# Two attentions on one core: a local score's eight places laid side by side, weight splits at other steps, and small VectorE pieces at other steps

## The chip, the core and the metric

The kernel runs on one core of a Trainium2 chip. The core has TensorE (PE in the profile: matrix products into PSUM), VectorE (DVE), ScalarE (ACT), GpSimd (POOL) and SyncE (SP, which here only issues transfers between HBM and SBUF). The engines run side by side. Each takes its own instructions strictly in the order in which the program gave them, and an instruction that waits for another engine holds up everything behind it on its own engine. The metric is the device time of one execution in microseconds (us).

## The reference

Two independent attentions over 2048 places with 576 columns, 32 heads of 18 columns; their outputs stand side by side.

```python
def _A_ref(x, wqkv, wo):              # local: 8 keys per place, at distances 0, 2, ... 14
    qkv = (x @ wqkv) ...              # q, k, v of 32 heads
    idx = pos[:, None] - off[None, :] ; mask = idx >= 0
    logits = einsum("bhsd,bhswd->bhsw", q, kg) * scale ; logits = where(mask, logits, -1e9)
    attn = softmax(logits, axis=-1)   # over the 8 keys
    return einsum("bhsw,bhswd->bhsd", attn, vg) ... @ wo
def _B_ref(x, wqkv, wo):              # full softmax attention of all 2048 places
    p = softmax(einsum("bhqd,bhkd->bhqk", q, k) * scale, axis=-1)
    return einsum("bhqk,bhkd->bhqd", p, v) ... @ wo
```

All of it is computed in float32 accuracy; products whose inputs matter most are taken of a high and a low half ("splits": `hi` is the rounded value and `lo` the rest).

## The kernel before

**The first part** (up to about 416 us of the trace) makes q, k and v of both attentions.

**The main loop** has 512 steps, and `step` counts them. B's heads stand in 8 groups of 4, and the queries in 4 blocks of 512; a step takes one group, one block and one of 16 key tiles of 128. So a block of queries has 16 steps, and ends in the steps whose number is a multiple of 16. In a plain step TensorE makes 4 score tiles of 128 x 512, makes 3 products more of the same kind for a later block (their maxima are subtracted from that block's scores), and multiplies the exponentials of the step before by v into the sums `po` (line 898). VectorE takes the maximum of each of the 3 products (lines 256, 258 and 272, tile `mx`), and ScalarE takes the exponentials of the 4 scores (lines 398 and 401). A product's PSUM bank is free again when its maximum has been taken. At a block's end VectorE also copies the sums: `o<-po`, line 908; in that step and the next it may have a reduction to one least value per query, `m<-mx` (line 282), and its transpose `mt<-m` (line 290).

**Attention A** runs beside this, in 8 blocks j of 256 places. Block j has `start = 10 + 55 * j`, and its pieces are placed at steps counted from there:

- `match` (lines 1042 and 1045, from step 5): GpSimd multiplies q with the keys at the 8 distances and adds over the columns. Its last addition, line 1049, writes the local scores `lg`, 128 partitions x 8 distances x 64 places.
- `most` (line 1059, steps 30 to 33): VectorE takes the maximum over the 8 distances, 16 places a piece, into `am`.
- `lower` (line 1065, step 33): GpSimd subtracts it. `exponents` (line 1069, steps 34 and 35, or all at 35 where step 35 also makes A's output): ScalarE. `total` (line 1076, step 36): GpSimd adds over the distances into `as`.
- `inverses` (line 1080, steps 37 and 38): VectorE, 32 places a piece. `share` (line 1083, step 38): GpSimd multiplies by them.
- `weighted` (lines 1090 to 1096, from step 38): GpSimd multiplies by v and adds; `upper` and `rest` (lines 1100 and 1105) split the result, which goes to HBM, comes back transposed, and is multiplied by A's output weights on TensorE in the steps that `TURNS` lists (line 1239; such a step takes about 4.1 us).

What sets the order is the table `agenda`: `plan(start, pieces)` puts each piece under a step's number, and `due()` runs what stands under the present step when TensorE's, VectorE's and ScalarE's own work of the step has been written. So a piece stands in its engine's queue behind that step's maxima, and there is no other scheduler. GpSimd's queue holds no work of the steps themselves: it runs ahead of the steps until a piece has to wait for another engine.

**Output weights.** `load_wo` (line 1000) loads 5 chunks of A's and of B's output weights into tiles `y` (four buffers, shared with the rows of the output) and, 3 steps later, splits each on GpSimd: a cast (line 176) and a subtraction (line 177). A's chunks are loaded at steps 28, 32, ... 44, B's at steps 404, 408, ... 420.

## Time and profile before

| what | value |
|---|---|
| median of 3 runs | 1580.74 us (1580.18 to 1582.28) |
| the profiled execution | 1580.53 us, its span 1578.7 us |
| busy share of the span | PE 99%, DVE 89%, ACT 75%, POOL 61% |
| granted TensorE clock | 1.00 |
| first `po` product of the main loop | 416.3 us |

The profiled execution's time is 1.8 us above its span, and 0.21 us under the median. A busy PE says little: its matmuls are pipelined and their ends are modelled. How long a step takes is seen in the chain of work that ended last, which lists the `po` products of each step with their start: a plain step is 2.00 us.

### The profile page before, as it was taken

To read this page: it belongs to the slowest core of one execution; us is meant where nothing else is said; L and a number is where in the kernel's file an instruction comes from. 1 tells how busy PE (TensorE), PEld (TensorE's weight loads), DVE (VectorE), ACT (ScalarE), POOL (GpSimd) and SP (SyncE) were. 2 spreads that over 40 slices of the span, in tenths; PEclk is the share of its full clock that TensorE was granted. 3 is DMA by queue.
4 is the path that set the end of the run, shared out by engine and by line. 5 is a ranking of instruction groups with operands and counts; after the bars stand their busy time and mean duration, and the time that the engine had idled before them with its cause. 6 is when DMAs were issued, how large, how long until landed. Compare 5 with 4: busy or idle time off the path is not lost.

```text
span 1578.7 us, 34691 instructions
## 1 busy us (share of the span) xinstructions
PE 1570.7 (99%) x13400; PEld 950.1 (60%) x13400; DVE 1397.6 (89%) x2381; ACT 1183.5 (75%) x1918; POOL 966.0 (61%) x820
## 2 busy tenths in 40 slices
PE   9999999999999999999999999999999999999998
PEld 7999998888544444445444445444444454555776
DVE  5299999999999999999999999999999999999433
ACT  7323441211699999999999999999999999898444
POOL 2305852201257997994996995995995997930100
PEclk9999999999999999999999999999999999999999
DMA  9848954523321253253235316423523142234211
GB/s 263 220 131 208 261 183 126 162 75 100 75 56 55 64 115 90 70 141 100 60 88 145 81 47 155 104 61 103 136 58 98 37 109 71 78 118 157 86 39 61
DMA packets 190149, 173.12 MB, mean 110 GB/s; under 512 B 123120, under 2 KB 136944, under 8 KB 188256
## 3 DMA queue, kind: packets, MB, share of 16 engines
q1 hardware_dynamic: 185120, 159.36, 36.3%
q0 software_dynamic: 4032, 10.63, 3.1%
q8 instruction: 105, 1.72, 0.5%
q10 hardware_dynamic: 832, 0.92, 0.2%
q14 instruction: 60, 0.49, 0.1%
HBM read 97.47 MB, written 72.95 MB: 108 GB/s over the span
## 4 chain that ended last, share of the span: by engine, by line
PE 96%; POOL 2%; DMA 1%; DVE 1%; issue 1%; ACT 0%; SPq 0%; POOLq 0%; ACTq 0%; DVEq 0%
PE po L898 31%; PE bank L239 19%; PE bank L498 16%; PE bank L388 10%; PE bank L1239 8%; PE pair L388 7%; PE bank L424 4%; POOL pr L1045 1%; POOL aohi L1042 0%; DMA first<-xb 0%; DMA raw<-wa 0%; DVE mx L256 0%; POOL ks L177 0%; POOL ohi L844 0%; DMA da<-ohi 0%
## 5 line engine op out<-in xcount | busy, mean ns | idle before, releaser
L239 PE MATMUL bank<-ks,qs 54*128 54x256 f32 (+1 forms) x2526 | 755.1, 372 | 1.3 <-DVE mx L256 0.6
L256 DVE TENSOR_REDUCE mx<-bank 128x1 f32<-128x512 f32 x1024 | 679.9, 684 | 59.5 <-PE bank L239 33.5
L239 PEld LDWEIGHTS bank<-ks,qs 54*128 54x128 f32 x2526 | 414.1, 184 | 428.4 <-DVE mx L272 312.5
L398 ACT ACTIVATE e<-bank 128x512 f32<-128x512 f32 x1024 | 611.2, 603 | 72.9 <-PE bank L388 66.0
L898 PE MATMUL po<-ee,v 128*19 128x512 f32 x2048 | 536.7, 599 | 0.0
L898 PE MATMUL po<-e,v 128*19 128x512 f32 x2048 | 531.4, 599 | 0.0
L401 ACT ACTIVATE ee<-pair 128x1024 f32<-128x1024 f32 x478 | 487.7, 1020 | 1.1 <-PE pair L388 0.4
L388 PE MATMUL bank<-qs,ks 56*128 56x512 f32 x1092 | 460.8, 441 | 0.0
L258 DVE TENSOR_REDUCE mx<-bank 128x2 f32<-128x512 f32 x546 | 355.8, 684 | 20.2 <-PE bank L239 7.2
L272 DVE TENSOR_REDUCE mx<-bank 128x2 f32<-128x512 f32 x478 | 326.1, 682 | 0.0
L388 PE MATMUL pair<-qs,ks 56*128 56x512 f32 x956 | 248.3, 396 | 0.0
L388 PEld LDWEIGHTS bank<-qs,ks 56*128 56x128 f32 x1092 | 194.4, 183 | 15.6 <-ACT e L398 7.1
L1090 POOL TENSOR_TENSOR pr<-lg,akv 128x1024 f32<-128x1024 f32 x72 | 157.2, 2205 | 0.6
L840 ACT ACTIVATE ohi<-bank 128x512 f32<-128x512 f32 (+1 forms) x56 | 30.6, 595 | 147.5 <-issue 125.5
L388 PEld LDWEIGHTS pair<-qs,ks 56*128 56x128 f32 x956 | 137.8, 185 | 0.0
L898 PEld LDWEIGHTS po<-ee,v 128*19 128x19 f32 x2048 | 69.6, 96 | 109.6 <-issue 109.6
L498 PE MATMUL bank<-xhi,ahi 64*128 64x512 f32 x448 | 116.1, 390 | 0.1
L498 PE MATMUL bank<-xlo,ahi 64*128 64x512 f32 (+1 forms) x448 | 104.1, 392 | 0.2 <-POOL xlo L546 0.2
L498 PE MATMUL bank<-xhi,alo 64*128 64x512 f32 x416 | 102.3, 390 | 0.0
L1042 POOL TENSOR_TENSOR pr<-aq,akv 128x1024 f32<-128x1024 f32 x40 | 87.7, 2199 | 17.0 <-PE bank L239 15.9
L1092 POOL TENSOR_TENSOR pr<-pr 128x512 f32<-128x512 f32 x72 | 91.3, 1293 | 0.6
L546 POOL TENSOR_TENSOR alo<-raw,ahi 128x512 fp32r<-128x512 f32 x13 | 16.8, 1294 | 113.1 <-ACT ahi L545 111.8
(210 smaller groups left out, 2369.5 us busy)
## 6 DMA issues: line engine op xcount, KB each, us to landing
do<-n SPq DMA_DIRECT2D x28, 512.0 KB
da<-ohi SPq DMA_DIRECT2D x52, 256.0 KB
akv<-da SPq DMA_DIRECT2D x64, 175.5 KB
out<-y SPq DMA_DIRECT2D x32, 288.0 KB
qs<-dqk SPq DMA_DIRECT2D x30, 288.0 KB
ks<-dqk SPq DMA_DIRECT2D x30, 288.0 KB
at<-dao SPq DMA_DIRECT2D x64, 128.0 KB
rec<-drec SPq DMA_DIRECT2D x29, 256.0 KB
```

What stands on the lines that cost most here:

```text
L239: return nc.tensor.matmul(ps, qs[rows_, b, p, 128 * t : 128 * t + 128], ks[rows_, p, 512 * k + at : 512 * k + at + n], start=True, stop=True)
L256: nc.vector.tensor_reduce(mx[:, r, p, t, k : k + 1], ps, axis=AX.X, op=ALU.max)
L258: nc.vector.tensor_reduce(mx[:, r, p, t, 2 * k - 2 : 2 * k], ps.rearrange("q (h n) -> q h n", h=2), axis=AX.X, op=ALU.max)
L272: nc.vector.tensor_reduce(mx[:, :, p, t, 2 * k - 2 + i], ps.rearrange("q (h n) -> q h n", h=2), axis=AX.X, op=ALU.max)
L388: nc.tensor.matmul(ps, ks[at, p, 128 * kt : 128 * kt + 128], qs[at, b, p], start=True, stop=True)
L398: nc.scalar.activation(e, ps, AF.Exp, scale=SCALE)
L401: nc.scalar.activation(whole, both_scores[0], AF.Exp, scale=SCALE)
L498: nc.tensor.matmul(ps, a, b, start=start, stop=stop)
L898: nc.tensor.matmul(po[32 * i : 32 * i + 19], vs[g][:, kt, 19 * i : 19 * i + 19], es[i], start=kt == 0, stop=kt == NT - 1)
L1090: nc.gpsimd.tensor_mul(at, ap(st["lg"], (0, 2), (SUB, W), (1, SUB)), window(st["v"], n))
L1092: nc.gpsimd.tensor_add(at[:, :, :4], at[:, :, :4], at[:, :, 4:])
L1239: nc.tensor.matmul(sums_[r], a, b, start=i == 0, stop=i == len(both[r]) - 1)
```

## The change

1. The last addition of `match` no longer writes `lg` (distance, place) but a tile `lgt` (place, distance), so that the 8 scores of a place stand side by side; the masked scores of block 0 are written there too. `most` reads them there: 8 neighbours per place instead of 8 values that lie 64 elements (256 bytes) apart. `lower` reads `lgt` with the distance outermost, that is 8 elements (32 bytes) from one place to the next, and writes `lg` in the old order; what follows is as before.
2. The inverses are taken in three pieces, of 22, 21 and 21 places, instead of two of 32, and so `share` and `weighted` stand one step later.
3. Pieces of `most` and `inverses` that fall on a step whose number is a multiple of 16 move behind it, and what follows moves with them. (The rule has a second case that no step here meets.) Worked out by hand from the new code: the maxima of block j = 1 move from steps 95 to 98 to 97 to 100; of j = 3 the fourth moves from 208 to 209; the inverses of j = 0 go from 47 and 48 to 49, 50 and 51, and of j = 7 from 432 and 433 to 433, 434 and 435. `share` moves by 3 steps in j = 0 and 1, by 2 in j = 3 and 7, and by 1 in the others.
4. A's output weights are loaded and split from step 2 on instead of step 28, B's from step 459 on instead of step 404.

```diff
             if c == DH // 2:
                 st["pr"] = st["prs"][0]
-                lg = st["lg"] = work.tile([128, W, SUB], F32, name="lg", bufs=1)
-                nc.gpsimd.tensor_add(lg, st["pr"][:, 0], st["pr"][:, 1])
+                st["lg"] = work.tile([128, W, SUB], F32, name="lg", bufs=1)
+                by = st["by"] = work.tile([128, SUB, W], F32, name="lgt", bufs=1)
+                nc.gpsimd.tensor_add(by.rearrange("p n w -> p w n"), st["pr"][:, 0], st["pr"][:, 1])
...
-            nc.vector.tensor_reduce(st[name][:, at], st["lg"][:, :, at].rearrange("p w n -> p n w"), axis=AX.X, op=op)
+            nc.vector.tensor_reduce(st[name][:, at], st["by"][:, at], axis=AX.X, op=op)
...
         def lower():
-            nc.gpsimd.tensor_sub(st["lg"], st["lg"], ap(st["am"], (0, W), (1, SUB)))
+            nc.gpsimd.tensor_sub(st["lg"], st["by"].rearrange("p n w -> p w n"), ap(st["am"], (0, W), (1, SUB)))
...
         def inverses(n):
-            half = st["as"][:, 0, SUB // 2 * n : SUB // 2 * n + SUB // 2]
-            nc.vector.reciprocal(half, half)
+            third = st["as"][:, 0, (0, 22, 43)[n] : (22, 43, SUB)[n]]
+            nc.vector.reciprocal(third, third)
...
-        INV = ((37, 0), (38, 1))
-        LOWER, SHARE, MATCH, WEIGHT = 33, 38, 5, 38
+        INV = ((37, 0), (38, 1), (39, 2))
+        LOWER, SHARE, MATCH, WEIGHT = 33, 39, 5, 39
+        start = A_FROM + GAP * j
+
+        def clear(at):
+            while (start + at) % NT == 0 or (start + at) % NT == 1 and start + at not in TURNS:
+                at += 1
+            return at
+
+        def apart_from_ends(pieces):
+            fit = []
+            for at, *args in pieces:
+                at = clear(max(at, fit[-1][0] + 1) if fit else at)
+                if not fit and clear(at + 1) > at + 1:
+                    at = clear(at + 1)
+                fit.append((at, *args))
+            return tuple(fit), fit[-1][0] - pieces[-1][0]
+
+        def behind_by(n, pieces):
+            return tuple((at + n, *args) for at, *args in pieces)
+
+        MOST, late = apart_from_ends(MOST)
+        EXPS, TOTAL, INV = (behind_by(late, p) for p in (EXPS, TOTAL, INV))
+        INV, more = apart_from_ends(INV)
+        LOWER += late
+        SHARE += late + more
+        WEIGHT += late + more
...
-        ("a", woa, 28, [[(0, 128 * c, 128)] for c in range(4)] + [[(64 * r, 512, 64) for r in range(2)]]),
-        ("b", wob, STEPS * (NG - 2) + 20,
+        ("a", woa, 2, [[(0, 128 * c, 128)] for c in range(4)] + [[(64 * r, 512, 64) for r in range(2)]]),
+        ("b", wob, STEPS * (NG - 1) + 11,
```

TensorE's order is the same in both kernels. What moves on the others is shown at two places. On VectorE, before, steps 207 and 208, in block j = 3 (`am` are the local maxima, `mx` the maxima of the steps' own products, `o<-po` the copy of the sums in step 208):

```order
L1059 TENSOR_REDUCE am<-lg 128x16
L282 TENSOR_REDUCE m_83<-mx 128x16
L256 TENSOR_REDUCE mx<-bank_12871 128x1
L272 TENSOR_REDUCE mx<-bank_12865 128x2
L256 TENSOR_REDUCE mx<-bank_12886 128x1
L908 COPY o<-po 128x512
L1059 TENSOR_REDUCE am<-lg 128x16
L290 STREAM_TRANSPOSE mt<-m_83 128x32
L256 TENSOR_REDUCE mx<-bank_12916 128x1
L256 TENSOR_REDUCE mx<-bank_12919 128x1
```

The same place of the changed kernel, from the copy in step 208 on into step 209:

```order
L908 COPY o<-po 128x512
L290 STREAM_TRANSPOSE mt<-m_83 128x32
L256 TENSOR_REDUCE mx<-bank_12921 128x1
L256 TENSOR_REDUCE mx<-bank_12924 128x1
L272 TENSOR_REDUCE mx<-bank_12911 128x2
L256 TENSOR_REDUCE mx<-bank_12944 128x1
L256 TENSOR_REDUCE mx<-bank_12954 128x1
L1143 TENSOR_TENSOR y<-bank_12930,y 128x288
L1060 TENSOR_REDUCE am<-lgt 128x16
L256 TENSOR_REDUCE mx<-bank_12994 128x1
```

The fourth maximum stood right behind the copy; now it stands in step 209, behind an addition for A's output (`y`), and `mt` and the step's `mx` follow the copy at once.

On GpSimd, before, the end of `match` of block j = 7, ahead of its maxima at steps 425 to 428 (`qs`, `ks` are the tiles into which B's output weights are split, from `y`):

```order
L176 CAST qs_3591<-y 126x576
L177 TENSOR_TENSOR ks_3592<-y,qs_3591 126x576
L997 MEMSET y 128x576
L1042 TENSOR_TENSOR aohi<-aq,akv 128x1024
L1045 TENSOR_TENSOR pr<-pr 128x1024
L1045 TENSOR_TENSOR pr<-pr,aohi 128x1024
L1049 TENSOR_TENSOR lg<-pr 128x512
L938 TENSOR_TENSOR n<-o,n 128x512
L176 CAST qs_3591<-y 128x576
L177 TENSOR_TENSOR ks_3592<-y,qs_3591 128x576
L1100 CAST aohi<-ao 128x1152
```

The same stretch of the changed kernel:

```order
L1042 TENSOR_TENSOR pr<-aq,akv 128x1024
L1045 TENSOR_TENSOR pr<-pr,aohi 128x1024
L936 TENSOR_TENSOR o<-o,rec 128x512
L937 CAST n<-o 128x512
L1042 TENSOR_TENSOR aohi<-aq,akv 128x1024
L1045 TENSOR_TENSOR pr<-pr 128x1024
L1045 TENSOR_TENSOR pr<-pr,aohi 128x1024
L1050 TENSOR_TENSOR lgt<-pr 128x8x64
L938 TENSOR_TENSOR n<-o,n 128x512
L1101 CAST aohi<-ao 128x1152
L1106 TENSOR_TENSOR ao<-ao,aohi 128x1152
```

The splits of B's output weights are gone from between the pieces of `match`, so that fewer instructions stand ahead of the local scores.

More of the change, by code (lines that the diff above doesn't have):

```diff
@@ L1047, in match @@
                 st["pr"] = st["prs"][0]
-                lg = st["lg"] = work.tile([128, W, SUB], F32, name="lg", bufs=1)
-                nc.gpsimd.tensor_add(lg, st["pr"][:, 0], st["pr"][:, 1])
+                st["lg"] = work.tile([128, W, SUB], F32, name="lg", bufs=1)
+                by = st["by"] = work.tile([128, SUB, W], F32, name="lgt", bufs=1)
+                nc.gpsimd.tensor_add(by.rearrange("p n w -> p w n"), st["pr"][:, 0], st["pr"][:, 1])
                 if j == 0:
                     for w in range(1, W):
-                        nc.gpsimd.memset(lg[:32, w, : DIL * w], MASKED)
+                        nc.gpsimd.memset(by[:32, : DIL * w, w], MASKED)
         def over_window(op, name, i, of):
@@ L1167, in local @@
         pieces += [(16 + 2 * i, lambda i=i: fetch("v", i)) for i in range(4)]
-        start = A_FROM + GAP * j
         for n in range(2):
```

## The prediction

> **What bounds the kernel now.** I read the page's chain, then the chain in order of time, stretch by stretch, and the timeline where the chain leaves TensorE.

> ```profile
> PE 96%; POOL 2%; DMA 1%; DVE 1%; issue 1%; ACT 0%; SPq 0%; POOLq 0%; ACTq 0%; DVEq 0%
> ```

> TensorE carries 96% of the chain. A change that leaves its work alone can only win the time by which some steps are longer than a plain one. The `po` products in the chain of waits show that; their columns are start, length and instruction. First an undisturbed block end (step 80 begins at 577.90) and an undisturbed one in which A's output is made (208 has this form; here it begins at 1192.96):

> ```profile
> 575.90 0.98 PE po L898 x8
> 577.90 0.99 PE po L898 x8
> 580.08 0.98 PE po L898 x8
> 582.07 0.99 PE po L898 x8
> ...
> 1192.96 0.98 PE po L898 x8
> 1197.05 0.98 PE po L898 x8
> 1199.04 0.98 PE po L898 x8
> ```

> So a plain step takes 2.00, the block end 2.18 and 1.99, the other 4.09 and 1.99. Now the four local maxima of j = 4, which meet nothing else; the maxima of j = 1 around the copy in step 96; those of j = 3 around step 208; and the inverses of j = 7 around step 432:

> ```profile
> 960.68 0.98 PE po L898 x8
> 962.69 0.98 PE po L898 x8
> 964.76 0.99 PE po L898 x8
> 966.85 0.98 PE po L898 x8
> 968.93 0.98 PE po L898 x8
> ...
> 610.35 0.99 PE po L898 x8
> 612.72 0.98 PE po L898 x8
> 614.73 1.05 PE po L898 x8
> 616.81 1.05 PE po L898 x8
> ...
> 847.27 0.98 PE po L898 x8
> 851.70 0.98 PE po L898 x8
> 853.85 0.98 PE po L898 x8
> ...
> 1335.23 0.98 PE po L898 x8
> 1337.70 0.98 PE po L898 x8
> ```

> In j = 4 the first maximum costs nothing (2.01), the next three 0.07, 0.09 and 0.08. In j = 1 the steps take 2.37, 2.01 and 2.08 where the undisturbed end had 2.18, 1.99 and 2.00. In j = 3 they take 4.43 and 2.15 against 4.09 and 1.99. In j = 7 one takes 2.47 against 2.18. The maxima of j = 7 are a case of their own; in the timeline, with the idle time before a row in brackets:

> ```profile
> 1318.14 0.39 DVE L1059 TENSOR_REDUCE am<-lg 128x16 f32<-128x128 f32 x1 [0.49 <-POOL lg L1049]
> 1318.16 1.01 PE L898 MATMUL po<-ee,v 128*19 128x512 f32 x2
> 1318.45 0.68 DVE L258 TENSOR_REDUCE mx<-bank 128x2 f32<-128x512 f32 x1
> 1319.05 0.68 DVE L272 TENSOR_REDUCE mx<-bank 128x2 f32<-128x512 f32 x1
> 1320.84 1.01 PE L898 MATMUL po<-ee,v 128*19 128x512 f32 x2
> ```

> Here VectorE waited 0.49 us for GpSimd's local scores, and the step became 2.68 long. These rows give VectorE's budget as well: maxima start 0.60 apart, so three take 1.80 of the 2.00, and 0.20 is left. The local maximum holds the queue for 0.31 (1318.14 to 1318.45): 2.11, which is the 0.07 to 0.09 seen in j = 4.

> **The change part by part.** *Neighbouring scores.* What the maximum costs in the new layout is not in the trace; the nearest rows by group (mean ns behind the bar) are:

> ```profile
> L1059 DVE TENSOR_REDUCE am<-lg 128x16 f32<-128x128 f32 x32 | 11.9, 373 | 0.5 <-POOL lg L1049 0.5
> L282 DVE TENSOR_REDUCE m<-mx 128x16 f32<-128x96 f32 x32 | 7.8, 243 | 0.4
> L1080 DVE RECIPROCAL as<-as 128x32 f32<-128x32 f32 x16 | 5.5, 343 | 0.0
> ```

> The least value `m` reads neighbours: 96 in 243 ns. A maximum `mx` reads 512 in 684 (the 0.68 above), so 1.06 ns an element, and 128 would take 277: 96 ns less than now. The bounds are 373 (no gain) and 243; I take 277, the row for neighbours being nearest. Then the slot is 0.31 - 0.10 = 0.21, three maxima and it make 2.01, and the 0.24 of such a place goes. I count it for j = 0, 2, 4, 5 and 6: 1.20. In j = 3 two of the three are plain, 0.16, and likewise in j = 7, 0.15.

> *Pieces away from the copy.* j = 1: 0.19 + 0.02 + 0.08 = 0.29 goes. j = 3: 0.34 + 0.16 = 0.50; the fourth maximum goes into step 209, behind A's output, where I cost it at nothing because a single small piece costs nothing (2.01 above). j = 7: 0.29 of the long step; its first inverse no longer stands between the copy and the next `mx`, but another still falls into that step, so I take 0.25. j = 0 gains nothing.

> *Three inverses.* A piece of 32 takes 343 ns, so one of 21 or 22 takes between two thirds of that, 229, and all of it: 0 to 0.34 more VectorE a block. None can be dearer than a maximum of 373, of which a single one cost nothing (2.01 above), and `share` waits for the last in any case. I take nothing; at 343 each, two in a row could cost 0.1 a block, 0.8 in all.

> *B's splits later.* By group on GpSimd:

> ```profile
> L176 POOL CAST qs<-y 126x576 fp32r<-126x576 f32 x4 | 2.7, 664 | 0.0
> L177 POOL TENSOR_TENSOR ks<-y,qs 126x576 fp32r<-126x576 f32 x4 | 5.7, 1421 | 0.3
> L1065 POOL TENSOR_TENSOR lg<-lg,am 128x512 f32<-128x512 f32 x8 | 10.2, 1281 | 42.9 <-DVE am L1059 42.9
> L177 POOL TENSOR_TENSOR mt<-mt 128x32 fp32r<-128x32 f32 x32 | 8.0, 251 | 2.6
> ```

> Four splits of 2.09 stood ahead of the scores of j = 7: 8.3 us. Against that `share` of j = 6 comes a step, 2.0, later. The scores are ready 6.3 us sooner, and the wait of 0.49 is gone: of the step's excess of 0.68 I take 0.67. Next late would be the first inverse, which waits for no such queue. The splits now run at the end of GpSimd's work, where it idles. On SP the five loads pass the transfers of A's last output rows and of B's kept outputs; the `y` buffers they take were last used four allocations earlier, so I cost them at nothing.

> *A's splits earlier.* 10.4 us of GpSimd move from its waits for `am` (42.9 us in all over seven blocks) into an idle stretch at the loop's start. One split stood before the first scores and one still does. Nothing.

> *Share later.* `share` of j = 0 moves by 3 steps, 6.0 us, and GpSimd has no pause between it and the next scores:

> ```profile
> 513.41 1.28 POOL L1083 TENSOR_TENSOR lg<-lg,as 128x512 f32<-128x512 f32 x1 [2.58 <-DVE as L1080]
> 605.39 1.30 POOL L1049 TENSOR_TENSOR lg<-pr 128x512 f32<-128x512 f32 x1
> 612.09 0.37 DVE L1059 TENSOR_REDUCE am<-lg 128x16 f32<-128x128 f32 x1
> ```

> One multiplication of 512 elements by `rec` (1.3, as long as `lower`) now runs in the wait ahead of `share`, so the scores of j = 1 are ready at 606.7 + 4.7 = 611.4. The first maximum now stands in the step in which the third did, at 612.09. It is 0.7 in time; a wait of up to 0.3 would follow if the write in the new order took 1 us more. I take 0.

> *The sum:* 1.20 + 0.16 + 0.15 + 0.29 + 0.50 + 0.25 + 0.67 = 3.22. The profiled execution, 1580.53, becomes 1577.3; it stands 0.21 under the median of the runs, so the forecast is 1577.5.

> **The price of `lower`, and the rivals.** `lower` now reads at 32 bytes distance. ScalarE's exponentials wait for it:

> ```profile
> 502.95 1.28 POOL L1065 TENSOR_TENSOR lg<-lg,am 128x512 f32<-128x512 f32 x1 [4.26 <-DVE am L1059]
> 503.89 0.60 ACT L398 ACTIVATE e<-bank 128x512 f32<-128x512 f32 x1
> 504.37 0.43 ACT L1069 ACTIVATE lg<-lg 128x256 f32<-128x256 f32 x1
> ```

> It ends at 504.23, 0.14 before ScalarE gets to them; a maximum shorter by 0.10 makes that 0.24. So stretches in four blocks (0, 1, 3 and 6; the others have a step more) hurt from 0.24 on, and ScalarE's queue behind it holds the next scores. Bounds from rows: its own 1.28, and 4.0 at the dearest price per element, 251/32 = 7.8 ns (`mt`) for 512. A gain is excluded, since it still writes as many elements as it reads. I take the near row, its own: nothing.

> *Rival 1: `lower` is some tenths longer.* Each 0.1 by which it grows beyond 0.24 costs 4 x 0.1. Between 1.6 and 2.3 us it gives back 0.3 to 3.1: 1577.8 to 1580.6, mostly within 0.2%. [...]

> *Rival 2: the maximum gets no cheaper.* Then 1.20 + 0.31 stay and part of the rest; about 1.5 is won: 1579.2. Against it stands the 243 ns row. [...]

> *Rival 3, slower: `lower` on ScalarE's path in full.* To end 3.2 us above the time before, it has to lose 6.4: 4 x (growth - 0.24) = 6.4, so from 3.1 us on. At the 4.0 of the dear row it loses 4 x 2.48 = 9.9: 1587.4. For it speaks only a 32-element row that is mostly fixed cost.

> *Rival 4:* SP is held by a late `y` buffer at steps 459 to 475, so that A's last transposed rows reach TensorE late. Those loads are issued 9 steps, 18 us, ahead. 1579 to 1584.

> **How the numbers follow.** A measurement of this kernel tells 0.2%, 3.2 us, from no change, and the forecast lies on that edge. The forecast's case, 1576.5 to 1578.5: 0.56, of which 0.40 beyond 0.2%. More steps freed than counted, down to 1575: 0.08. Rival 1: 0.14; rival 2: 0.10; rival 3: 0.08; rival 4: 0.04. That makes faster 0.48, same 0.16 + 0.14 + 0.10 = 0.40, slower 0.12. The range 1575.2 to 1581.0 takes in all but rivals 3 and 4.

> **What would show it.** `am` at 0.28 us, and steps of 2.00 in j = 4; no idle time of VectorE before the first `am` of j = 7 nor of j = 1; 4.1 at step 208; `lower` below 1.5. The forecast is wrong if ScalarE waits for `lower`, if `am` stays at 0.37, or if VectorE waits for the scores of j = 1.

## The result: 0.39% slower, with a gain of about the forecast's size inside it

The changed kernel takes 1587.55 us (median of 8 runs, 1585.34 to 1589.58), the kernel before on the same chip 1580.77. The ratio is 1.0039 (95% interval 1.0030 to 1.0047), 6.8 us slower where 3.2 us faster was forecast. Ratios here are formed from undisturbed executions alone, against the kernel before on the same chip, and they need not equal the quotient of two medians. The profiled execution of the changed kernel is the longest of its eight: 1589.58, span 1587.8.

In what follows a step is numbered as in the expectations, by the interval between the starts of its `po` products. The block end of the prediction that lasted from 577.90 to 580.08 is step 81 in that count.

Most of the signs that the forecast named came; one did not, `lower` below 1.5 us. The groups of the changed kernel (mean ns behind the bar; L1060 is the local maximum, L1066 `lower`, L1050 the write of the local scores, L1081 one third of an inverse):

```profile
L1060 DVE TENSOR_REDUCE am<-lgt 128x16 f32<-128x128 f32 x32 | 8.8, 274 | 0.0
L1066 POOL TENSOR_TENSOR lg<-lgt,am 128x512 f32<-128x512 f32 x8 | 12.3, 1543 | 53.0 <-DVE am L1060 53.0
L1050 POOL TENSOR_TENSOR lgt<-pr 128x512 f32<-128x512 f32 x8 | 10.4, 1296 | 0.6
L1081 DVE RECIPROCAL as<-as 128x21 f32<-128x21 f32 x16 | 4.4, 277 | 0.0
```

The maximum takes 274 ns instead of 373, and `lower` 1.54 us. The steps that held the maximum are plain again or nearer to it, as the chain of waits shows: two steps of j = 4, then steps 97 and 208 with their neighbours.

```profile
973.90 0.98 PE po L898 x8
975.90 0.98 PE po L898 x8
977.91 0.98 PE po L898 x8
...
614.46 0.98 PE po L898 x8
616.61 0.98 PE po L898 x8
...
858.81 0.98 PE po L898 x8
862.98 0.98 PE po L898 x8
```

The steps of j = 4 are 2.00 and 2.01 where they were 2.07 to 2.09, step 97 is 2.15 instead of 2.37, step 208 is 4.17 instead of 4.43 (4.1 was forecast). Against that stand two stalls that the kernel before does not have. The chain of the changed kernel in order of time (start, length, what), around step 81 and around step 144:

```profile
568.61 13.33 DMA ks<-dqk
582.18 0.47 PE bank L239
582.65 1.34 PE po L898 x8
585.79 1.37 PE po L898 x8
588.18 0.98 PE po L898 x8
...
712.97 8.11 DMA at<-dao
721.21 1.57 PE bank L1264 x10
725.52 1.48 PE po L898 x8
728.02 0.98 PE po L898 x8
```

TensorE's own rows there, with the idle time before each and what ended it by the profile:

```profile
579.97 0.47 PE L239 MATMUL bank<-ks,qs 54*128 54x512 f32 x1 [1.14 <-DVE mx L258]
582.18 0.47 PE L239 MATMUL bank<-ks,qs 54*128 54x512 f32 x1 [1.28 <-DMA ks<-dqk]
718.52 0.40 PE L1264 MATMUL bank<-wohi,at 64*128 64x288 f32 x2 [3.07 <-DMA at<-dao]
721.21 0.61 PE L1264 MATMUL bank<-wohi,at 64*128 64x288 f32 x2 [2.29 <-DMA at<-dao]
```

TensorE waits for the loaded rows of `ks` of the next group at step 81, and for A's loaded rows `at` at step 144. The first of the four pauses is put down to a maximum on VectorE, but that maximum had ended at 579.02, 0.95 us before TensorE went on. An earlier load of `ks` is the likelier cause; it is not shown in this profile. By the starts of the `po` products, steps 80 to 85 take 16.79 us where they took 12.19, steps 143 to 147 take 20.34 where they took 12.11: 4.60 and 8.23, together 12.83 us. The rest of the loop is 3.69 us shorter. The profiled execution before was 1580.53; with 12.83 more and 3.69 less that makes 1589.67, against the 1589.58 of this one.

A part of each stall comes after its wait. The busy time by stretch of the changed kernel, two rows around the first stall and two around the second. Behind the length of the stretch stand the busy time of PE, PEld (the loading of weights), DVE, ACT and POOL, each with its number of instructions, then the granted clock of TensorE, the busy share of the DMA engines and their GB/s:

```profile
579.73:583.14 3.41, 1.89 (x14) 0.83 (x14) 1.74 (x3) 1.51 (x2) 3.33 (x3) 1.00 0.32 101
583.20:586.50 3.30, 3.30 (x18) 1.51 (x16) 1.71 (x4) 1.64 (x3) 3.22 (x2) 0.50 0.54 125
716.26:719.67 3.41, 0.40 (x2) 0.22 (x2) 1.27 (x3) 0.02 (x1) 3.35 (x2) 1.00 0.69 143
719.80:726.40 6.60, 5.19 (x37) 3.96 (x37) 1.84 (x3) 1.46 (x3) 4.64 (x3) 0.50 0.72 188
```

TensorE pauses with its clock at 1.00, and then works at 0.50 for a while. That is why the eight `po` products above last 1.34, 1.37 and 1.48 instead of 0.98.

### The profile page after: what moved, and what is told of

Read it like the earlier page. It is cut to its first block, busy times and chain, and to the rows that moved or that the text cites. A ratio compares the mean times of both kernels' runs of the same rounds, so it can differ in the third digit from the quotient of the medians.

```text
span 1587.8 us, 34701 instructions
## 1 busy us (share of the span) xinstructions
PE 1572.2 (99%) x13400; PEld 950.3 (60%) x13400; DVE 1394.4 (88%) x2389; ACT 1183.5 (75%) x1918; POOL 968.2 (61%) x820
## 4 chain that ended last, share of the span: by engine, by line
PE 95%; DMA 2%; issue 1%; DVE 1%; POOL 0%; ACT 0%; SPq 0%; ACTq 0%; DVEq 0%; POOLq 0%
PE po L898 31%; PE bank L239 19%; PE bank L498 16%; PE bank L388 10%; PE bank L1264 8%; PE pair L388 7%; PE bank L424 4%; DMA ks<-dqk 1%; DMA qs<-dqk 1%; DMA at<-dao 1%; PE bank L664 0%; DMA da<-ohi 0%; DVE mx L256 0%; POOL ohi L844 0%; SPq L216 0%
## 5 line engine op out<-in xcount | busy, mean ns | idle before, releaser
L398 ACT ACTIVATE e<-bank 128x512 f32<-128x512 f32 x1024 | 611.4, 603 | 74.5 <-PE bank L388 64.3
L898 PE MATMUL po<-ee,v 128*19 128x512 f32 x2048 | 538.0, 600 | 0.0
L898 PE MATMUL po<-e,v 128*19 128x512 f32 x2048 | 532.7, 600 | 0.0
L258 DVE TENSOR_REDUCE mx<-bank 128x2 f32<-128x512 f32 x546 | 355.6, 683 | 19.9 <-PE bank L239 6.4
L272 DVE TENSOR_REDUCE mx<-bank 128x2 f32<-128x512 f32 x478 | 325.6, 681 | 0.0
L898 PEld LDWEIGHTS po<-ee,v 128*19 128x19 f32 x2048 | 69.6, 96 | 110.1 <-issue 110.1
L652 POOL TENSOR_TENSOR olo<-olo,ohi 128x512 fp32r<-128x512 f32 x36 | 46.1, 1293 | 67.3 <-ACT ohi L651 55.8
```

The source lines that it names most:

```text
L258: nc.vector.tensor_reduce(mx[:, r, p, t, 2 * k - 2 : 2 * k], ps.rearrange("q (h n) -> q h n", h=2), axis=AX.X, op=ALU.max)
L272: nc.vector.tensor_reduce(mx[:, :, p, t, 2 * k - 2 + i], ps.rearrange("q (h n) -> q h n", h=2), axis=AX.X, op=ALU.max)
L398: nc.scalar.activation(e, ps, AF.Exp, scale=SCALE)
L898: nc.tensor.matmul(po[32 * i : 32 * i + 19], vs[g][:, kt, 19 * i : 19 * i + 19], es[i], start=kt == 0, stop=kt == NT - 1)
```

## Where the late loads come from

The rows of SyncE's queue and of GpSimd tell it. First SyncE in the kernel before, then in the changed kernel (start, time the issues take, instruction): the store of the negated maxima, the last four `ks` loads of the group at step 81, then the store and the second pair of `at` loads for step 144.

```profile
550.17 1.17 SPq L300 DMA_DIRECT2D dm<-mt  x2
558.01 6.81 SPq L215 DMA_DIRECT2D ks<-dqk  x4
673.25 1.19 SPq L300 DMA_DIRECT2D dm<-mt  x2
698.28 1.90 SPq L1118 DMA_DIRECT2D at<-dao  x2
```

```profile
554.31 1.14 SPq L300 DMA_DIRECT2D dm<-mt  x2
562.13 6.74 SPq L215 DMA_DIRECT2D ks<-dqk  x4
683.26 1.20 SPq L300 DMA_DIRECT2D dm<-mt  x2
712.01 1.32 SPq L1119 DMA_DIRECT2D at<-dao  x2
```

In the first place the store is issued 4.1 us later, and so are the loads behind it in the queue. In the second the store is 10.0 us later and the loads are 13.7; step 144 itself begins only 3.8 us later (713.61 against 709.78), which is the first stall less what was won. `dm<-mt` waits for the halves `mt` that GpSimd makes: it is issued 0.26 us after their cast starts in the kernel before (550.17 against 549.91), 0.23 in the changed kernel (554.31 against 554.08). On GpSimd, first before, then changed:

```profile
549.91 0.23 POOL L176 CAST mt<-mt 128x32 fp32r<-128x32 f32 x1
```

```profile
518.93 1.28 POOL L1084 TENSOR_TENSOR lg<-lg,as 128x512 f32<-128x512 f32 x1 [9.22 <-DVE as L1081]
554.08 0.20 POOL L176 CAST mt<-mt 128x32 fp32r<-128x32 f32 x1
```

`share` of j = 0 started at 513.41 after an idle time of 2.58 (quoted in the prediction); now it starts at 518.93 after 9.22, waiting for the last third of the inverse, and the halves 35 us further on in GpSimd's queue are 4.2 us late. So the theory was: three steps' delay of `share` in j = 0 and j = 1 make GpSimd late, GpSimd holds SyncE at `dm<-mt`, and the loads behind it reach TensorE too late.

## The experiments

| kernel | median us | ratio to before on the same chip, 95% interval | stall at 81, 144 (us over the kernel before) |
|---|---|---|---|
| layout alone | 1578.82 | 0.9995, 0.9984 to 1.0005 | none |
| pieces alone | 1594.13 | 1.0077, 1.0064 to 1.0090 | 5.4, 4.8, a third at 426 |
| splits alone | 1579.56 | 0.9992, 0.9983 to 1.0000 | none |
| layout and splits | 1577.59 | 0.9977, 0.9969 to 0.9986 | none |
| changed, j = 0 and 1 as before | 1577.57 | 0.9978, 0.9969 to 0.9987 | none |
| before, `share` of j = 0 later | 1581.22 | 1.0007, 0.9998 to 1.0015 | none |
| before, `share` of j = 1 later | 1580.56 | 0.9997, 0.9988 to 1.0006 | none |
| changed, `dm<-mt` later | 1578.33 | 0.9984, 0.9975 to 0.9993 | none |
| before, inverses of j = 0 three steps later | 1586.13 | 1.0029, 1.0017 to 1.0040 | 5.2, none |
| before, inverses of j = 1 three steps later | 1587.02 | 1.0038, 1.0025 to 1.0052 | none, 4.8 |
| before, inverses of j = 1 two steps later | 1584.50 | 1.0020, 1.0011 to 1.0029 | none, 3.4 |
| the eighth, exponentials a step later too | 1578.23 | 0.9985, 0.9975 to 0.9994 | none |

The last column is the length of steps 80 to 85 and of steps 143 to 147 less that of the kernel before (12.19 and 12.11), in the one profiled execution of each. In two of these executions the part ahead of the loop was longer too, where no edit acts: by 3.1 us with the layout alone, and by 4.4 us with the inverses of j = 1 two steps later. So their whole times, 1581.72 and 1588.69, say nothing of the stalls.

**The three parts apart.** The layout alone is the kernel before with these lines:

```diff
-                nc.gpsimd.tensor_add(lg, st["pr"][:, 0], st["pr"][:, 1])
+                by = st["by"] = work.tile([128, SUB, W], F32, name="lgt", bufs=1)
+                nc.gpsimd.tensor_add(by.rearrange("p n w -> p w n"), st["pr"][:, 0], st["pr"][:, 1])
...
-            nc.vector.tensor_reduce(st[name][:, at], st["lg"][:, :, at].rearrange("p w n -> p n w"), axis=AX.X, op=op)
+            nc.vector.tensor_reduce(st[name][:, at], st["by"][:, at], axis=AX.X, op=op)
...
-            nc.gpsimd.tensor_sub(st["lg"], st["lg"], ap(st["am"], (0, W), (1, SUB)))
+            nc.gpsimd.tensor_sub(st["lg"], st["by"].rearrange("p n w -> p w n"), ap(st["am"], (0, W), (1, SUB)))
```

> The kernel before with only the new order of the local scores (lgt): maxima of neighbours, the subtraction reading at 32 bytes distance; no piece and no split moves. Theory 1 (the loss of the changed kernel comes from share and what follows it standing later in GpSimd's queue): no stall near steps 81 and 144, granted clock 1.00 throughout; about 1.5 us won by the cheaper maxima, 0.3 to 0.5 lost where ScalarE waits for the longer subtraction: 1579.6. Theory 2 (the new tile or the strided passes on GpSimd cause the loss): 1585 to 1589, with the two stalls. Theory 3 (TensorE's clock is halved at times by itself, whatever the kernel): a clock below 1.00 here as well.

No stall. The time is within the measurement of the kernel before. Its loop is 1.83 us shorter, by the starts of the first and the last step's `po` products. The next kernel is the changed one with the old layout and the old starts of the splits, so that only the moved maxima and inverses are left:

```diff
-        ("a", woa, 2, [[(0, 128 * c, 128)] for c in range(4)] + [[(64 * r, 512, 64) for r in range(2)]]),
-        ("b", wob, STEPS * (NG - 1) + 11,
+        ("a", woa, 28, [[(0, 128 * c, 128)] for c in range(4)] + [[(64 * r, 512, 64) for r in range(2)]]),
+        ("b", wob, STEPS * (NG - 2) + 20,
```

> The changed kernel without the new order of the scores and without the moved splits: only the pieces of maxima and inverses, share and weighted stand at the new steps. Theory 1: both stalls are there (4.7 us at steps 81 to 83 and 8.2 us at 144 and 145 in the changed kernel's profile), about 1.0 us is won elsewhere: 1588 to 1592, clock below 1.00 at the two places. Theory 2: no stall, 1579.7. Theory 3: as in any other run.

Both stalls are there, and a third at steps 426 and 427: the scores of j = 7, still behind B's splits, are late by 2.42, as VectorE's timeline of this kernel shows (idle time in brackets).

```profile
1330.07 0.38 DVE L1059 TENSOR_REDUCE am<-lg 128x16 f32<-128x128 f32 x1 [2.42 <-POOL lg L1049]
```

The moved pieces alone thus cost 13 us, and 1594.13 lies above the expected 1588 to 1592, since the third stall was not foreseen. The splits alone, which are the two lines above the other way round in the kernel before:

> The kernel before with only the splits of the output weights moved. Theory 1: the wait of 0.49 us before the first maximum of block 7 is gone and its step is 0.67 shorter, nothing else: 1580.1. Theory 2b (the earlier loads and splits of A's weights push GpSimd's queue late and cause the loss): 1585 to 1589.

The wait at j = 7 is gone and nothing is late. Layout and splits together, every piece where it was:

> The changed kernel with every piece at its old step and two inverses: new order of scores and moved splits alone. Theory 1: no stall, 1.5 us of the maxima and 0.67 of block 7 won, 0.3 to 0.5 lost to ScalarE: 1578.8, clock 1.00. Theory 2: the loss stays, 1585 or more.

1577.59 is the forecast's time, 0.23% under the kernel before, but that is luck: the pieces, which the forecast counted as 1.04 us of gain (0.29, 0.50 and 0.25), are not in this kernel. In the changed kernel they cost 10 us on top of this. So for these four theory 1 holds, and theories 2, 2b and 3 fall.

**Only j = 0 and j = 1.** In the changed kernel the moves are left out for these two:

```diff
...
-        MOST, late = apart_from_ends(MOST)
-        EXPS, TOTAL, INV = (behind_by(late, p) for p in (EXPS, TOTAL, INV))
...
+        if j > 1:
+            MOST, late = apart_from_ends(MOST)
+            EXPS, TOTAL, INV = (behind_by(late, p) for p in (EXPS, TOTAL, INV))
...
+        else:
+            INV, SHARE, WEIGHT = ((37, 0), (38, 1)), 38, 38
```

> The changed kernel, but with j = 0 and j = 1 left as they were: two inverses, nothing moved, the shares at steps 48 and 103 in place of 51 and 106. Theory 1 (the shares of j = 0 and j = 1, three steps later, make the two stalls): both stalls go, 4.75 us at steps 81 to 83 and 8.25 us at steps 144 and 145 of the changed kernel's 1587.55 us; lost with them is the 0.3 us that j = 1's moved maxima gain, so 1574.8 to 1577.6 us, and a granted clock of 1.00 at both places. Theory 4 (the stalls come from any of the moved pieces, those of j = 2 to 7 too, or from the splits): at least one of the stalls stays, 1580 us or more.

Both stalls go with these two blocks, and the granted clock is 1.00 at both places. With 1577.57 this kernel and the one with layout and splits alone beat the kernel before by 0.22 to 0.23%, and the changed kernel by more. Between these two the moved pieces and the third inverses of j = 2 to 7 are the difference. Their medians are the same, and in the profile the loop with the pieces is 0.25 us shorter, where the forecast counted 0.75 for j = 3 and j = 7. So even without the stalls the moved pieces win next to nothing.

**`share` later: a miss.** In the kernel before, for one block (j = 0; j = 1 in the other kernel):

```diff
         LOWER, SHARE, MATCH, WEIGHT = 33, 38, 5, 38
+        if j == 0:
+            SHARE, WEIGHT = 41, 41
```

> The kernel before, with the share and the weighted values of j = 0 alone three steps later (51 in place of 48); maxima, inverses and splits as before. Theory 1 says that the place of the stall goes with the block of local attention that is late: a stall of 3 to 5 us at steps 81 to 83, none at 144, 1583.5 to 1586.5 us. Theory 4 (it takes the inverses and maxima of the changed kernel as well): no stall, 1580 to 1581.5 us.

> The kernel before, with the share and the weighted values of j = 1 alone three steps later (106 in place of 103). Theory 1: no stall at step 81, one of 4 to 8.5 us at steps 144 and 145, 1584.5 to 1589.5 us. Theory 4: no stall, 1580 to 1581.5 us.

No stall in either, against the theory. GpSimd's timeline with `share` of j = 0 three steps later shows why:

```profile
514.02 1.28 POOL L1083 TENSOR_TENSOR lg<-lg,as 128x512 f32<-128x512 f32 x1 [1.32 <-DVE as L1080]
549.12 0.20 POOL L176 CAST mt<-mt 128x32 fp32r<-128x32 f32 x1
```

It still starts where it did, 513.41 then and 514.02 now (in this profile the loop itself begins 0.58 later), and only one other instruction has passed it. The table of steps gives GpSimd an order, not a time. Written three steps later, `share` still started when what it reads was there, after an idle time of 1.32 us that ended with the inverse of VectorE, and that had not moved. So not the later `share` is the cause, but the inverse for which it waits.

**The inverse later.** The next three kernels move the inverse with it (j = 0, three steps; j = 1, three; j = 1, two), in the kernel before:

```diff
+        if j == 0:
+            INV, SHARE, WEIGHT = ((40, 0), (41, 1)), 41, 41
```

> The kernel before, with the two inverses of j = 0 three steps later (50 and 51 in place of 47 and 48), and the share and the weighted values with them; all else as before. Theory 1b (what GpSimd has to wait for is the inverse: its queue is only an order, so a share written later starts when it did, but an inverse made later by VectorE leaves GpSimd idle, and everything behind in its queue comes later, the halves of the maxima too): the share starts in step 51 or 52, its idle time ahead grows by about 6 us, the halves come 2 steps later than step 67, and a stall of 3 to 5 us stands at steps 81 to 83 and none at 144: 1583.5 to 1586.5 us. Theory 6 (the later inverse alone doesn't do it; it takes the new layout or the splits as well): no stall, 1580 to 1581.5 us.

> The kernel before, with the two inverses of j = 1 three steps later (105 and 106 in place of 102 and 103), and the share and the weighted values with them. Theory 1b: no stall at 81, one of 4 to 8.5 us at steps 144 and 145, 1584.5 to 1589.5 us. Theory 6: no stall, 1580 to 1581.5 us.

> As the run before, but the inverses of j = 1 only two steps later (104 and 105). Theory 1b: the store of the maxima and the loads behind it are issued 2 us sooner than with three steps, so the stall at 144 is shorter by about 2 us, or by more if it takes a clock of half speed with it: 0 to 5 us, 1580.5 to 1586 us, below the run with three steps. Theory 6: no stall, 1580 to 1581.5 us.

Each stall follows its own block, and in j = 1 its length follows the delay: 3.4 us with two steps, 4.8 with three, each from one profile; the medians, 1584.50 and 1587.02, go the same way. The 5.2 us of j = 0 are a little above the expected 3 to 5. GpSimd with the inverses of j = 0 later:

```profile
519.59 1.28 POOL L1083 TENSOR_TENSOR lg<-lg,as 128x512 f32<-128x512 f32 x1 [7.19 <-DVE as L1080]
554.77 0.22 POOL L176 CAST mt<-mt 128x32 fp32r<-128x32 f32 x1
```

GpSimd idles 7.19 us instead of 2.58 ahead of `share`, and the halves come 4.9 us later (0.35 of it because the loop itself begins later in this profile). These two blocks, one at a time and with no new layout and no moved split, give the sign and about the size of the result. Only the place in between was still argued: that the delay reaches TensorE through SyncE's queue.

**SyncE's queue.** The changed kernel, all its pieces as late as they are, with the store four steps later and the load behind it three:

```diff
-            later(1 if g == NG - 1 else 2, lambda: order(parts))
+            later(1 if g == NG - 1 else 6, lambda: order(parts))
...
-            later(1 if g == NG - 1 else 3, place)
+            later(1 if g == NG - 1 else 2, place)
```

> The changed kernel with every share as late as it is there, but the store of the negated maxima (dm<-mt, L300) four steps later in the agenda, and the load behind it (qs<-dm, L306) three steps later: SyncE comes to the store when GpSimd has long made the halves, and the loads that stood behind it in its queue are issued at their time. Theory 1a (SyncE's queue held at that store makes TensorE wait, for ks<-dqk at step 81 and for at<-dao at step 144): both stalls go, 1574.5 to 1577.5 us, though GpSimd is as late as in the changed kernel. Theory 5 (the late halves themselves, or GpSimd's late weighted values, reach TensorE by another way than SyncE's queue): the stalls stay or grow, 1586 us or more.

Its SyncE, the cast of its `mt` on GpSimd, and the chain around step 81:

```profile
549.25 1.57 SPq L215 DMA_DIRECT2D ks<-dqk  x4
554.47 1.23 SPq L300 DMA_DIRECT2D dm<-mt  x2
555.79 5.30 SPq L215 DMA_DIRECT2D ks<-dqk  x2
```

```profile
554.19 0.25 POOL L176 CAST mt<-mt 128x32 fp32r<-128x32 f32 x1
```

```profile
577.59 0.99 PE po L898 x8
579.77 0.98 PE po L898 x8
581.77 0.98 PE po L898 x8
```

The halves are as late as in the changed kernel (the cast starts at 554.08 there and at 554.19 here), but four of the six `ks` loads are issued ahead of the store, at 549.25, and the last two have been issued by 561.09, where the kernel before ended at 564.82. Step 81 is 2.18 again. For step 144 the second pair of `at` loads is issued at 701.16 (712.01 in the changed kernel). Both stalls are gone, and 1578.33 is 9.2 us below the changed kernel. That shows the queue to be the way. The time is still above the expected 1574.5 to 1577.5, and 0.8 us above the kernel with j = 0 and 1 as before, on the same chip; where these 0.8 us stand was not followed up.

**What the exponentials cost.** In the changed kernel, and in the one just described, the steps 45, 102, 211 and 375 of the blocks with two exponentials are 0.16 to 0.20 too long. That could be the longer `lower`, whose end the first exponential awaits. So in these blocks the exponentials and everything behind them were put one step later again:

```diff
+        if len(EXPS) == 2:
+            EXPS, TOTAL = ((35, 0, 2), (36, 1, 2)), ((37, 0), (37, 1), (37, 2))
+            INV, SHARE, WEIGHT = ((38, 0), (39, 1), (40, 2)), 40, 40
```

> The kernel of the run with the later store of the maxima, and in the blocks with two exponentials (j = 0, 1, 3 and 6) the exponentials, the totals and the inverses one step later again, so that ScalarE comes to the first exponential when the lowered scores (1.54 us instead of 1.28) have long been written. Theory 7 (the 0.16 to 0.19 us by which the steps 45, 102, 211 and 375 are long there are ScalarE's wait for the lowered scores): the first of the two steps with exponentials falls to 0.10 us of excess or less in each of the four, 0.3 to 0.5 us in all, 1577.7 to 1578.2 us, which the time alone can't tell and the steps can. Theory 8 (the exponentials themselves make both steps long, whenever they stand): the excess only moves by a step, 1578.0 to 1578.7 us.

The excess only moved by a step, from 45 and 46 to 46 and 47, as the chain of this kernel shows from the start of step 45 on (2.00, 2.19, 2.19):

```profile
504.80 0.98 PE po L898 x8
506.80 0.98 PE po L898 x8
508.99 0.98 PE po L898 x8
511.18 0.99 PE po L898 x8
```

So theory 7 falls: it isn't a wait for `lower`. ScalarE's timeline in the kernel with the later store shows the cost itself:

```profile
500.81 1.02 ACT L401 ACTIVATE ee<-pair 128x1024 f32<-128x1024 f32 x1
502.81 1.02 ACT L401 ACTIVATE ee<-pair 128x1024 f32<-128x1024 f32 x1
504.19 0.43 ACT L1070 ACTIVATE lg<-lg 128x256 f32<-128x256 f32 x1
504.98 1.04 ACT L401 ACTIVATE ee<-pair 128x1024 f32<-128x1024 f32 x1
507.14 1.07 ACT L401 ACTIVATE ee<-pair 128x1024 f32<-128x1024 f32 x1
```

Its steps begin 2.00 apart without a local exponential and 2.17 and 2.16 apart with one (the second, at 506.36, isn't shown), with no idle time between. In the kernel before, the first of the two exponentials of j = 0 fell into the row of steps that the maxima had made 2.08 to 2.12 long, and only one step, 46, was 0.19 too long. That those longer steps gave ScalarE its room is argued, not shown.

## Why the prediction was wrong

**What bounds the kernel.** Right: TensorE, and only steps longer than plain ones could be won from. What was not asked is which of the plain steps were plain by a narrow margin.

**Share later, the step that failed.** The prediction followed `share` to one reader, the next local scores, found them 0.7 us in time, and wrote "I take 0". It even saw that `share` of j = 0 would be 6 us later and that GpSimd has no pause behind it. But 35 us behind it in the same queue stand the halves `mt`; SyncE waits for them at `dm<-mt`, and behind that store stand `ks` of the next group and A's rows. That order could have been read in the profile before. How small the margin was there is an estimate with the changed kernel's help. In the changed kernel the last `ks` transfer lands 13.07 us after its four issues end (568.61 and 13.33 against 562.13 and 6.74). The same four end at 564.82 before, which puts the landing at an estimated 577.9, and TensorE's step 81 began at 577.90 with its first use of the new group inside it: a margin of about 2 us at most, under a delay of 4.1. The two stalls cost 12.83 us in the profile. The instruction to ask about was the inverse, not `share`: in "Three inverses" stands that `share` "waits for the last in any case", and this wait was priced at nothing.

**Neighbouring scores.** Right: 274 ns against the 277 taken. In the kernel with the layout alone the windows of j = 0, 2, 4, 5 and 6 are 0.16, 0.27, 0.26, 0.25 and 0.16 us shorter, 1.10 against 1.20 counted. The shortfall is in j = 0 and j = 6, two of the blocks with two exponentials. The same 128 elements take 373 ns where the 8 values of a place lie 256 bytes apart and 274 where they are neighbours.

**Pieces away from the copy.** j = 1 gave 0.24 (0.29 counted with nothing else in it). j = 3 was mis-sized: 0.24 in all where 0.16 and 0.50 were counted, and less than the 0.35 that the layout alone gave there. The long step 208 did become 4.17, but the fourth maximum in step 209 pushed the exponentials a step on, and steps 211 and 212 became 0.17 and 0.19 too long, where 209 and 211 had been 0.15 and 0.04. j = 7 with its layout, its inverse and the splits gave 1.14 against 1.07, and of that the splits alone 0.63 against 0.67. The inverses of j = 0 in a place without a copy gave 0.12 that was not counted.

**Splits.** At the places asked about they were right. In the profile with the splits alone, and in that of the changed kernel, the steps outside all these windows are 0.5 to 0.6 us shorter in sum (steps 240, 357 and 444 are 0.17 to 0.21 shorter each, while 327 is longer by 0.18). That gain was put at nothing, and its cause was not looked for.

**`lower`.** Taken at 1.28, it is 1.54. It grew by 0.26, just over the 0.24 from which it was said to hurt, and the last experiment shows that the time lost there isn't its own. Reading at 32 bytes distance thus costs this subtraction a fifth more, 1543 ns against 1281.

**Rivals.** Rivals 2 and 3 did not come, and rival 1 hardly: `lower` is longer, but with 1.54 us below its 1.6. That rival 3's highest figure, 1587.4, stands next to the measured time is chance, since it asked for a `lower` of 4.0 us. Rival 4, with 4 in 100, had the right last link of the second stall, SyncE held and A's rows late for TensorE, but another holder (a `y` buffer) and another place (steps 459 to 475). The slower side got 0.12, two thirds of it for `lower`.

In sum: the terms that were counted as 3.22 made 2.72 by the figures above (1.10, 0.24, 0.24 and 1.14), and about 1 us more came from where nothing had been counted, so that 3.69 lies near the forecast is in part luck. One term, put at zero, was 12.8 us.

## What to carry to other kernels

Before a small piece is moved later, list every instruction that the waiting engine has behind it in its queue up to the next point with slack, and for each store among those that another queue issues, list what stands behind that store too. A table of steps sets an order: whether a later place costs anything depends on whether what it reads comes later (`share` of j = 0 alone three steps later left no stall, with its inverses it left one of 5.2 us), so ask for the producer, not for the place. And a TensorE pause of a few microseconds is to be priced above its own length: here pauses of 2.42 us stood in a stall of 4.60, and pauses of 5.36 in one of 8.23, with the clock at 0.50 after them.

## What the runs showed that was not expected

**The clock after a pause.** TensorE's clock, 1.00 in the kernel before from 5.6 us to the end of its span, went to 0.50 behind every stall, for 3.41 us or 6.83: from 583.14 for 3.41 and from 719.68 for 6.83 in the changed kernel (its mean granted clock is 0.996), in the kernel with the pieces alone from 581.23 for 6.83, from 721.18 for 3.41 and from 1332.16 for 3.41 (mean 0.996), and for 3.41 each at the stalls of the three kernels with later inverses (means 0.999, 0.999 and 0.998). In the last of these, j = 1 two steps later, it did so ahead of the loop as well, from 77.24 for 3.41. The pauses were short: at step 81 of the changed kernel TensorE idled 1.14 and 1.28 us with work between, at step 144 3.07 and 2.29.

What such a stretch costs was not tried apart from the pause. As an estimate from these rows, 3.41 us at half speed hold 1.7 us of work less; pauses of 2.42 and that make 4.1 of the 4.60 us of the first stall.

**A strided write for nothing.** GpSimd writes the scores 32 bytes apart in 1296 ns and wrote them side by side in 1285 (L1049 before), while reading them so takes 1543 against 1281.
